# Moving the early weight splits and the first batch's routing to other slots of an attention pipeline, and dividing the weight conversions of the first experts differently

## The chip, the cores and the metric

The kernel runs on one core of a Trainium2 chip. TensorE (PE; its weight loads are PEld) multiplies matrices, VectorE (DVE), ScalarE (ACT) and GpSimd (POOL) do elementwise work, and SyncE (SP) starts most of the DMA transfers. The metric is the device time of one execution in microseconds (us).

## The reference

Three stages follow each other, all in float32:

```python
q_assign = argmax(normalised q @ normalised centroids)      # 16 clusters a head; k_assign alike
scores = where(q_assign == k_assign, q @ k.T / 8, -1e9)     # 2 batches x 8 heads, 768 x 768, D = 64
x = softmax(scores) @ v                                     # as 1536 tokens of 512
logits = normalised x @ normalised expert_emb.T / tau       # 8 experts
e = argmax(logits);  gate = softmax(logits)[e]
x = gate * (relu(x @ w1[e]) @ w2[e])                        # 512 -> 1024 -> 512, one expert a token
h = x @ w_in                                                # 512 -> 2048
out = (P(h) / (Q(h) + 1e-6)) @ w_out                        # P cubic, Q from |h| and h*h
```

## The kernel before, in words

The operands of most products are split into a high part in the type fp32r (hi) and a rest (lo = value - hi), and a product is made as hi x hi + lo x hi + hi x lo, or a part of that.

**Attention.** One unit is half of the queries (3 blocks of 128) of one head; there are 32 units. A unit has six key blocks kb, so the program runs through 192 slots t = 6 u + kb. Everything in a slot is written out by hand; `at(slot, function, ...)` puts other work into a slot. The order in a slot is: transposes of the probabilities into pt (L463), `word_high`, the exponential (L454), the parts phi and plo of the transposed block (L471 and L481 on ScalarE and VectorE; for kb = 0 GpSimd makes both, L72 and L479), the finishing of the unit before (px, L523), the other tasks, the products with v (L491, L492), and last one step of the running routing. The sums of a unit (ssum, L503) and the values' parts (vhl, L363) are GpSimd's too.

The transposes (pt), the scores (ps) and the output (po_acc) have PSUM banks of their own; one more bank, of the pool pM, is shared in turn by all that comes up rarely: the words (cm), the cluster logits (pl, L373 in the first two heads and L380 later) and the turned one-hots (po, L428), px, and the routing's products pr_ (L585) and ptab (L618). Who takes that bank has to wait until its user before has been read.

**Words.** The FFN's weights are prepared during the attention in 32 pieces ("words"): GpSimd makes the low half (L232, L234), ScalarE the high half into the bank cm (L239), VectorE joins the two into a buffer wz (L244), and a store writes it away. Two or three words fall to a period of 12 slots.

**Routing.** After the last head of a batch each half of the batch is routed to the experts: a chain of small VectorE operations (L563 to L580) makes a one-hot (rohb), TensorE counts the rank within the expert (pr_, L585), VectorE and GpSimd make J and at_row (L605 to L613), and TensorE turns them into the table of rows (ptab, L618). `advance_one` does the next step in chosen slots, steps that take the shared bank in slots of their own. The rows of x are stored to xd in DRAM as they are ready, and an indirect DMA on GpSimd (L658) gathers the rows of one expert by row_tok.

**Expert 0's first block.** The first 128 rows of expert 0 come from batch 0 alone, so they are worked on inside the end of the attention (names that begin with eb): `eb_gather`, `eb_ids`, `eb_x` (turned rows, ebx), `eb_in` (products with w1, L674, in the last eight slots and behind them), `eb_relu`, `eb_h`, `eb_low`, `eb_out` (products with w2, L689), `eb_end`. The weights come as four chunks of expert 0 (w1 in chunks 0 and 1, w2 in 2 and 3), each of 4 quarters of 128x512. `early_hi` makes a quarter's hi part, `early_lo` its lo part (L197), `early_split` both. `load_ahead(n)` starts the load of chunk n into one of three raw buffers (wraw, L129).

**The experts behind it.** `block_in`, `block_turn` (turned h; hhi L681, hlo L682) and `block_out` do expert 0's second 128 rows, `transpose_x(1)` turns expert 1's rows, and then a loop of steps (e = 1..7, p = 0..3) does the rest. `weights(k)` converts the next k quarters (ScalarE casts, L112, then VectorE subtracts, L117) into a ring of eight chunks. `row_gates` and `positions` are generators that the loop advances once a step; the second step of `positions` multiplies and copies the counts (pi, then pin, L1100). Afterwards comes the FFN, the second half of the run.

The lines that decide in which slots the routing of batch 0 advances, and where the early splits stand, are:

```python
            elif t % (2 * NB) in (1, 3, 7, 9):
                advance_one(t % (2 * NB) == 1)
            at((165, 170, 172, 177)[j], early_split, 0, j, pool, pool)
            at(186 + j, early_split, 1, j, act, pool)
            at(190 + j, early_hi, 2, j, act)
```

Of the kernel before, what the change touches and what calls it, by code (L numbers as in the profile page):

```python
# [10 lines left out]
F32 = mybir.dt.float32  # L11
# [10 lines left out]
P = 128  # L22
# [6 lines left out]
def attention_moe_kernel(ctx: ExitStack, tc: tile.TileContext, kqT, vp, centroids,  # L29
# [313 lines left out]
    def prep_split_first(i, qk):  # L343
# [11 lines left out]
        dve.tensor_copy(KB[D:P], qk[D:P])  # L355
# [77 lines left out]
    units = [(i, g) for i in range(NH) for g in range(2)]  # L433

# [81 lines left out]
    def finish(u):  # L516
        i, g = units[u]
        b, h = heads[i]
        px = (pS.tile([P, 3, D + E], F32, name="px", tag="ps") if u == n - 1 else
              pM.tile([P, 3, D + E], F32, name="px", tag="pm"))  # L520
        ob = st["ob", u]
        for j in range(3):
            pe.matmul(px[:, j, :], ob[:, j * P:(j + 1) * P], JE[:, h, :], start=True, stop=True)  # L523
        if h == 0 and g == 0:
# [12 lines left out]
        else:  # L537
            dve.tensor_tensor(x_sb[:, g * 3:g * 3 + 3, h * D:(h + 1) * D], px[:, :, 0:D],
                              r.to_broadcast([P, 3, D]), op=ALU.mult)
        if h == H - 2:  # L540
            dve.tensor_reduce(lg2[:, rows, :, 1], lg[:, rows], axis=AX.X, op=ALU.add)
            store_x(b, g, slice(0, h * D + D))
# [81 lines left out]
    def first_rows_1():  # L624
        tot = pM.tile([P, E], F32, name="ptot", tag="pm")
        pe.matmul(tot[:, 0:1], onesb, cum[:, 0:1], start=True, stop=True)
        dve.tensor_copy(e0[:, 0:1], tot[:, 0:1])
# [66 lines left out]
    def eb_gather():  # L694
        eb["x"] = hp.tile([P, S], F32, name="kq", bufs=4)[:, 0:W]
        gather_x(eb["x"], 0, NT // B + 1)

    def eb_ids():
        eb["y"] = hp.tile([P, S], F32, name="kq", bufs=4)[:, 0:W]
# [6 lines left out]
        eb["gates"] = gate(eb["gate"], eb["x"].unsqueeze(1), 1,  # L706
                           (ss, mx.unsqueeze(2), small[:, 128:128 + E].unsqueeze(1), sq))

    def eb_gate():
        next(eb["gates"], None)  # L710

    def eb_x():
# [4 lines left out]
        eb["ph"] = pS.tile([P, 2, 512], F32, name="ebh", tag="ps")  # L717

    def eb_in(j, first=0, upto=3 * KC):
        block_in(eb["ph"][:, j], eb["xT"], j, first, upto)  # L720

    def eb_relu(j):
        eb["hr", j] = hp.tile([P, 512], F32, name=f"wz{3 * j}", bufs=1)
        act.activation(eb["hr", j], eb["ph"][:, j], AF.Relu)
# [16 lines left out]
    def eb_end():  # L741
        act.activation(eb["y"][:, 0:DM], eb["o"], AF.Copy, scale=eb["gate"][:, 0:1])
# [39 lines left out]
    for j in range(15):  # L782
        for w0, w1_ in ((7, 11), (8, 17)) + (((9, 13),) if j in (9, 12) else ()):
# [32 lines left out]
    with tc.manual_schedule():  # L816
# [55 lines left out]
        cl_logits_first(1)  # L872
# [5 lines left out]
        cl_onehot(0)  # L878
        norm_1(embs, E, junk[:E, :], acc[:E, 2:3])
        cl_max(1)  # L880
        cl_transp_first(0)
# [70 lines left out]
        for j in range(4):  # L952
            at((165, 170, 172, 177)[j], early_split, 0, j, pool, pool)
# [640 lines left out]
```

## Time and profile before

| | |
|---|---|
| three runs | 770.41, 771.95, 773.9 us; median 771.95 |
| the profiled execution | 771.65 us, of which the span (first to last instruction) is 769.9 |
| attention | to about 305 us |
| experts | from there to about 500 us |
| FFN | to the end |

Busy time is the time in which an engine worked at an instruction. TensorE's matrix products are pipelined, so its instructions can overlap. A wait is idle time of an engine ahead of an instruction, with the instruction that ended it behind the arrow. The granted clock of a stretch is given as a share of full speed (1.00).

### The profile page before, as it was taken

Reading aid. Unit: us, or ns where it says so; the run is one execution under the profiler, and the core shown is the slowest. Engines: PE = TensorE matmul, PEld = TensorE weight load, DVE = VectorE, ACT = ScalarE, POOL = GpSimd, SP = SyncE. Lnnn points to the kernel's source line nnn. Section 1 sums busy time; section 2 is a strip of 40 time slices with the busy share of each in tenths; the row PEclk is TensorE's granted clock in tenths of the full one; section 3 lists DMA queues with packets and bytes.
Section 4 is the critical chain, followed back from the end, with each engine's and each line's share of the span. In section 5 each row is a group of like instructions: output and inputs, shape, how many; then the busy total and the mean of one; then the engine's idle time right before and its main releaser. Section 6 shows DMA issues by size and latency. Waiting matters only on the chain.

```text
span 769.9 us, 12566 instructions
## 1 busy us (share of the span) xinstructions
PE 734.6 (95%) x4261; PEld 636.2 (83%) x4261; DVE 591.5 (77%) x1125; ACT 567.1 (74%) x1131; POOL 368.0 (48%) x461
## 2 busy tenths in 40 slices
PE   6899999999999989989999999999999999999996
PEld 5789999998888877779889999878788888888885
DVE  6778888888898885578965655589987878788774
ACT  4778888888887893667875556588877677777774
POOL 7498888888777864102211012166544532242220
PEclk9999999999999999999999999999999999999999
DMA  5576776866777345479876656223000200010001
GB/s 146 158 205 176 197 218 195 241 183 211 237 251 242 101 161 169 149 277 321 264 265 199 213 184 202 82 77 103 14 1 14 69 16 13 0 56 1 0 1 58
DMA packets 48712, 109.20 MB, mean 142 GB/s; under 512 B 6937, under 2 KB 10777, under 8 KB 48642
## 3 DMA queue, kind: packets, MB, share of 16 engines
q1 hardware_dynamic: 45618, 98.65, 40.8%
q0 software_dynamic: 2880, 9.55, 4.2%
q8 instruction: 35, 0.57, 0.3%
q14 instruction: 35, 0.29, 0.1%
q10 hardware_dynamic: 144, 0.13, 0.1%
HBM read 76.06 MB, written 18.99 MB: 123 GB/s over the span
## 4 chain that ended last, share of the span: by engine, by line
PE 76%; DVE 8%; ACT 5%; issue 4%; DMA 3%; POOL 3%; SPq 0%; ACTq 0%; POOLq 0%; DVEq 0%
PE pg L1245 14%; PE ph L1174 9%; PE pt L463 6%; PE pr L1414 5%; PE pr L1412 5%; PE pr L1413 5%; PE po_acc L491 3%; PE ps L445 3%; PE ps L446 3%; PE po_acc L492 3%; PE py L1205 3%; PE py L1203 3%; PE py L1204 3%; PE px L523 3%; PE pl L380 2%
## 5 line engine op out<-in xcount | busy, mean ns | idle before, releaser
L1272 POOL TENSOR_TENSOR Bt<-Bt,A 128x512 f32<-128x512 f32 x46 | 59.7, 1298 | 147.2 <-ACT Bt L1270 147.2
L481 DVE TENSOR_TENSOR plo<-pt,phi 128x384 fp32r<-128x384 f32 x160 | 88.1, 551 | 24.2 <-ACT phi L471 21.8
L463 PE MATMUL pt<-ident,pr 128*128 128x128 f32 x576 | 96.2, 276 | 3.5 <-DVE plo L481 2.7
L471 ACT CAST phi<-pt 128x384 fp32r<-128x384 f32 x160 | 76.7, 482 | 30.9 <-PE pt L463 29.7
L448 DVE TENSOR_REDUCE nm<-ps 128x1 f32<-128x768 f32 x96 | 91.2, 950 | 5.4 <-PE ps L446 5.2
L1245 PE MATMUL pg<-x2hi,ck 128*128 128x512 f32 x368 | 92.7, 394 | 2.4 <-DVE Ct L1273 2.4
L454 ACT ACTIVATE pr<-ps,nm 128x768 f32<-128x768 f32 x96 | 87.3, 910 | 2.8 <-DVE nm L448 2.3
L1245 PEld LDWEIGHTS pg<-x2hi,ck 128*128 128x128 f32 x368 | 68.8, 188 | 19.1 <-DVE Ct L1273 3.7
L463 PEld LDWEIGHTS pt<-ident,pr 128*128 128x128 f32 x576 | 70.9, 140 | 16.4 <-DVE plo L481 7.1
L117 DVE TENSOR_TENSOR ck<-wraw,ck 128x512 fp32r<-128x512 f32 x112 | 70.8, 685 | 15.4 <-ACT ck L112 15.2
L1412 PE MATMUL pr<-ck,ghi 128*128 128x512 f32 x192 | 76.1, 396 | 0.0
L1414 PE MATMUL pr<-ck,glo 128*128 128x512 f32 x192 | 75.5, 393 | 0.0
L1413 PE MATMUL pr<-ck,ghi 128*128 128x512 f32 x192 | 75.3, 392 | 0.0
L491 PE MATMUL po_acc<-phi,vhl 128*128 128x384 f32 x192 | 73.4, 382 | 0.0
L640 POOL TENSOR_TENSOR gss<-gss,half 128x2 f32<-128x2 f32 (+1 forms) x8 | 6.2, 780 | 131.4 <-ACT px L639 114.9
L112 ACT CAST ck<-wraw 128x512 fp32r<-128x512 f32 x112 | 62.1, 624 | 9.4 <-DMA wraw<-in_w_dram 9.3
L492 PE MATMUL po_acc<-plo,vhl 128*128 128x384 f32 x192 | 65.0, 339 | 0.0
L1174 PE MATMUL ph<-xhi,ck 128*128 128x256 f32 x448 | 62.6, 282 | 0.0
L1389 DVE SCALAR_TENSOR_TENSOR Bt<-Bt,A 128x512 f32<-128x512 f32 (+1 forms) x48 | 32.7, 682 | 37.3 <-ACT A L1388 37.0
L1174 PEld LDWEIGHTS ph<-xhi,ck 128*128 128x128 f32 x448 | 59.0, 188 | 2.2
L1387 ACT ACTIVATE A<-Bt,qc 128x512 f32<-128x512 f32 (+1 forms) x48 | 34.3, 715 | 22.5 <-POOL Bt L1272 22.5
L1245 PE MATMUL pg<-x2lo,ck 128*128 128x512 f32 x184 | 49.9, 392 | 0.0
(328 smaller groups left out, 1941.1 us busy)
## 6 DMA issues: line engine op xcount, KB each, us to landing
wraw<-in_w_dram SPq DMA_DIRECT2D x32, 1024.0 KB, 5.8
words<-in_w_in_dram SPq DMA_DIRECT2D x16, 512.0 KB, 6.3
wf_d<-wz SPq DMA_DIRECT2D x32, 256.0 KB, 3.5
words<-in_w_out_dram SPq DMA_DIRECT2D x16, 512.0 KB, 5.2
yraw<-wf_d SPq DMA_DIRECT2D x16, 512.0 KB, 4.1
operands<-operands SPq DMA_DIRECT2D x40, 192.0 KB, 2.7
kq<-in_kqT_dram SPq DMA_DIRECT2D x16, 384.0 KB, 5.5
ys_d<-ysb SPq DMA_DIRECT2D x15, 260.0 KB, 3.8
```

Source lines behind the costliest of these rows:

```text
L448: dve.tensor_reduce(nm, ps[:, :, :HS], axis=AX.XY, op=ALU.max, negate=True)
L454: act.activation(pr.rearrange("p (a s) -> p a s", a=2), ps[:, :, :HS], AF.Exp, bias=nm[:, 0:1], accum_out=st["sum", u][:, qb:qb + 1])
L463: pe.transpose(t[:, j, :], st["P", u][j][:, kb * P:(kb + 1) * P], ident)
L471: act.copy(phi, tv)
L481: dve.tensor_tensor(plo, tv, phi.bitcast(F32), op=ALU.subtract)
L491: pe.matmul(o, w, phi, start=(kb == 1), stop=False)
L492: pe.matmul(o, w, plo, start=False, stop=(kb == 0))
L1174: pe.matmul(ph[:, f2, :], w[:, wx, k, c0:c0 + P], x[:, k, :], start=(i == 0), stop=(i == len(ops) - 1))
L1245: pe.matmul(ph, w[:, wx, k, c0:c0 + P], x[:, k, :], start=(i == 0), stop=(i == len(ops) - 1))
L1412: pe.matmul(o, ghi[:, s_], w[:, 0, k, :], start=(fb == 0), stop=False)
L1413: pe.matmul(o, ghi[:, s_], w[:, 1, k, :], start=False, stop=False)
L1414: pe.matmul(o, glo[:, s_], w[:, 0, k, :], start=False, stop=(fb == F2B - 1))
```

## The change

It moves work between slots and changes a few engines; nothing is computed differently.

1. At the start head 0's one-hot is turned (`cl_transp_first(0)`) ahead of head 1's cluster logits; the copy to KB goes from VectorE to ScalarE.
2. The two words of j = 14 (slots 168 to 187) are gone from there; two words more take third places in the periods j = 3 and 6, and join in slots 49 and 85, as others do at 121 and 157 already.
3. The routing of batch 0 advances in more slots: all odd ones but those of kb = 5, and t mod 12 = 4 and 10; steps that take the bank in t mod 6 = 1. By counting the steps, pr_ and ptab stand at slots 109 and 115 for the first half and 133 and 139 for the second (before: 121 and 133, 145 and 157). The count ptot is made in the bank of unit 22's px; the gather, ebx and the ids are 10, 11 earlier and 6 later (slots 147, 163, 165); the block's gate leaves the slots and goes behind the attention as `eb_gate_1` to `_3`.
4. Chunk 0 is split at slots 165, 167, 170, 173; chunk 1 wholly on GpSimd at 175 to 181 (before: ScalarE and GpSimd at 186 to 189); chunk 2's hi on ScalarE at 183 to 187, its lo on GpSimd at 184 and 186 and on VectorE at 187 and 188; chunk 3's lo on VectorE behind the gate. Load 3 is at slot 174, loads 4 and 5 at 187 and 191, load 6 ahead of `eb_out(0, 8)`.
5. The rows x and y of expert 0's block lie in a tile of their own (spare_x), the halves of its h in two PSUM tiles (ebh), and the final scale goes to VectorE.
6. Behind the attention 16 quarters are converted ahead of the loop of steps, before 8; the generator `positions` starts its second step at i = 5, before at i = 2.

```diff
-        dve.tensor_copy(KB[D:P], qk[D:P])
+        act.copy(KB[D:P], qk[D:P])
...
+        bank_ = (pS.tile([P, 512], F32, name="px", tag="ps") if u == n - 1 else
+                 pM.tile([P, 512], F32, name="px", tag="pm"))
+        px = bank_[:, 0:3 * (D + E)].rearrange("p (j d) -> p j d", d=D + E)
...
+        if u == UF:
+            tot = bank_[:, 500:501]
+            pe.matmul(tot, onesb, cum[:, 0:1], start=True, stop=True)
...
     def eb_gather():
-        eb["x"] = hp.tile([P, S], F32, name="kq", bufs=4)[:, 0:W]
+        spare = xpool.tile([P, NB, W], F32, name="spare_x", tag="x_sb")
+        eb["x"], eb["y"] = spare[:, 0], spare[:, 1]
...
+    def eb_gate_1():
+        ss, mx, v, sq = eb["gates"]
+        act.activation(sq, eb["x"][:, 0:DM], AF.Square, accum_out=ss)
+        pool.tensor_tensor(ss, ss, half, op=ALU.pow)
+
+    def eb_gate_2():
+        ss, mx, v, sq = eb["gates"]
+        dve.tensor_reduce(mx, eb["x"][:, DM:W], axis=AX.X, op=ALU.max)
+        dve.tensor_tensor(v, eb["x"][:, DM:W], mx.to_broadcast([P, E]), op=ALU.subtract)
+        dve.tensor_scalar(ss, ss, 1e-6, None, op0=ALU.add)
+        dve.reciprocal(ss, ss)
...
     def eb_in(j, first=0, upto=3 * KC):
-        block_in(eb["ph"][:, j], eb["xT"], j, first, upto)
+        if first == 0:
+            eb["ph", j] = (pT if j else pS).tile([P, 512], F32, name="ebh", tag="pt" if j else "ps")
+        block_in(eb["ph", j], eb["xT"], j, first, upto)
...
-        act.activation(eb["y"][:, 0:DM], eb["o"], AF.Copy, scale=eb["gate"][:, 0:1])
+        dve.tensor_scalar(eb["y"][:, 0:DM], eb["o"], eb["gate"][:, 0:1], None, op0=ALU.mult)
...
-    for j in range(15):
-        for w0, w1_ in ((7, 11), (8, 17)) + (((9, 13),) if j in (9, 12) else ()):
+    for j in range(14):
+        for w0, w1_ in ((7, 11), (8, 17)) + (((9, 13),) if j in (3, 6, 9, 12) else ()):
...
-            at((165, 170, 172, 177)[j], early_split, 0, j, pool, pool)
-            at(186 + j, early_split, 1, j, act, pool)
-            at(190 + j, early_hi, 2, j, act)
-        for j in range(2):
-            at(192 + j, early_lo, 2, j, pool)
-            at(T + j, early_hi, 3, j, act)
-        at(178, load_ahead, 3)
-        at(134, first_rows_1)
-        at(136, first_rows_2)
-        at(157, eb_gather)
-        at(159, eb_ids)
...
+            at((165, 167, 170, 173)[j], early_split, 0, j, pool, pool)
+            at((175, 177, 179, 181)[j], early_split, 1, j, pool, pool)
+            at((183, 185, 186, 187)[j], early_hi, 2, j, act)
+            at((184, 186, 187, 188)[j], early_lo, 2, j, dve if j > 1 else pool)
+        at(174, load_ahead, 3)
+        at(187, load_ahead, 4)
+        at(191, load_ahead, 5)
...
+            elif t % 2 and t % NB != 5 or t % (2 * NB) in (4, 10):
+                advance_one(t % NB == 1)
...
+        weights(4)
         block_in(ph[0], x1, 0)
         act.activation(hr[0], ph[0], AF.Relu)
-        weights(2)
+        weights(1)
         block_in(ph[1], x1, 1, 0, 6)
         block_turn(0)
+        weights(2)
         block_in(ph[1], x1, 1, 6)
...
-            if i == 1:
+            if i == 4:
                 later.append(place_rows)
```

GpSimd, the last slots of the attention before: the five subtractions in a row (ck with its number is one chunk; 4461 is chunk 1, 4533 chunk 2), then the routing's J.

```order
L503 TENSOR_SCALAR ssum<-ssum 128x3
L72 TENSOR_SCALAR phi<-ptc 128x384
L479 TENSOR_TENSOR plo<-ptc,phi 128x384
L197 TENSOR_TENSOR ck_4461<-wraw,ck_4461 128x512 x4
L197 TENSOR_TENSOR ck_4533<-wraw,ck_4533 128x512
L612 TENSOR_TENSOR rJ<-rot,rsec 128x24
L613 TENSOR_TENSOR rJ<-rot,rJ 128x24
```

The same place of the changed kernel (4267 is chunk 1, 4412 chunk 2; its lines are numbered a few higher):

```order
L72 TENSOR_SCALAR ck_4267<-wraw 128x512
L197 TENSOR_TENSOR ck_4267<-wraw,ck_4267 128x512
L504 TENSOR_SCALAR ssum<-ssum 128x3
L197 TENSOR_TENSOR ck_4412<-wraw,ck_4412 128x512
L72 TENSOR_SCALAR phi<-ptc 128x384
L480 TENSOR_TENSOR plo<-ptc,phi 128x384
L197 TENSOR_TENSOR ck_4412<-wraw,ck_4412 128x512
L619 TENSOR_TENSOR rJ<-rot,rsec 128x24
```

Chunk 1 has moved ahead, hi parts and all, and one subtraction of chunk 2 stands between the last phi/plo pair and J.

VectorE, from the last unit but one's finishing to the one-hot of the last but one routing, before:

```order
L481 TENSOR_TENSOR plo<-pt,phi 128x384 x2
L531 TENSOR_TENSOR lg_2678<-px,rr 128x24
L538 TENSOR_TENSOR x_sb<-px,rr 128x3x64
L563 TENSOR_TENSOR x_sb<-lg_2678 128x3x8
L567 TENSOR_REDUCE rmx<-x_sb 128x3
L569 TENSOR_TENSOR rv<-x_sb,rmx 128x24
```

And after:

```order
L197 TENSOR_TENSOR ck_4412<-wraw,ck_4412 128x512
L501 TENSOR_SCALAR ssum<-ssum 128x3
L509 RECIPROCAL rr<-ssum 128x3
L482 TENSOR_TENSOR plo<-pt,phi 128x384
L197 TENSOR_TENSOR ck_4412<-wraw,ck_4412 128x512
L482 TENSOR_TENSOR plo<-pt,phi 128x384
L536 TENSOR_TENSOR lg_2697<-px,rr 128x24
```

Two subtractions of chunk 2 have come in between the plo operations, ahead of the routing; before they stood behind row_tok.

VectorE in the loop of steps around the copy to pin, before:

```order
L117 TENSOR_TENSOR ck_5087<-wraw,ck_5087 128x512 x2
L650 TENSOR_SCALAR gate<-gmx_4900 128x2
L651 RECIPROCAL gate<-gate 128x2
L1100 COPY pin<-px_5094 128x8
L666 TENSOR_TENSOR xlo<-px_5132,xhi 128x4x128
```

And after:

```order
L117 TENSOR_TENSOR ck_5266<-wraw,ck_5266 128x512 x2
L117 TENSOR_TENSOR ck_5304<-wraw,ck_5304 128x512
L1204 SCALAR_TENSOR_TENSOR hlo<-ph,hhi 128x512
L117 TENSOR_TENSOR ck_5304<-wraw,ck_5304 128x512 x3
L1121 COPY pin<-px_5335 128x8
```

The copy still stands behind weight subtractions, but of a later chunk, three steps later in the loop.

## Rows read from the trace of the kernel before

**Rows 1.** The page, TensorE: busy time, share of the span, instructions.

```profile
PE 734.6 (95%) x4261; PEld 636.2 (83%) x4261; DVE 591.5 (77%) x1125; ACT 567.1 (74%) x1131; POOL 368.0 (48%) x461
```

**Rows 2.** Windows of units: length; busy us and instructions of each engine; clock; DMA.

```profile
91.00:97.90 6.90, 6.90 (x49) 6.58 (x48) 6.18 (x14) 6.81 (x17) 5.58 (x13) 1.00 0.75 220
...
97.90:107.01 9.11, 9.10 (x67) 8.32 (x66) 7.17 (x14) 7.21 (x17) 8.45 (x12) 1.00 0.58 168
...
272.71:279.70 6.99, 6.89 (x47) 6.18 (x46) 6.42 (x15) 6.65 (x17) 2.44 (x4) 1.00 0.87 284
```

**Rows 3.** TensorE's waits: total us, times, longest.

```profile
PE px L664 <- DVE pin L1100: 2.9, 1, 2.9
...
PE pr__4558 L585 <- DVE rohb L577: 2.8, 1, 2.8
...
PE pr__3024 L585 <- DVE wz L244: 1.4, 1, 1.4
...
PE ptab L618 <- DVE wz L244: 1.4, 1, 1.4
...
PE py L689 <- ACT hhi L681: 1.1, 1, 1.1
...
PE ebh L674 <- ACT wz L724: 0.7, 1, 0.7
...
PE px L523 <- DVE e L627: 0.6, 1, 0.6
...
PE ebx L664 <- PE ps L446: 0.6, 1, 0.6
```

**Rows 4.** Timelines of the start: start, length, engine, line, operands, [idle before].

```profile
10.46 2.77 PE L373 MATMUL pl<-CB,kq 128*128 128x32 f32 x12 [1.37 <-POOL kq L324]
...
11.73 0.28 ACT L411 ACTIVATE oh<-oh 128x96 bf16<-128x96 bf16 x1
...
13.16 1.45 PE L428 MATMUL po<-identb,oh 128*16 128x128 bf16 x12
...
33.22 0.83 POOL L324 TENSOR_SCALAR kq<-kq 64x768 f32<-64x768 f32 x1 [5.62 <-DMA kq<-in_kqT_dram]
```

**Rows 5.** Groups by line: busy us, mean ns of one, idle before.

```profile
L197 POOL TENSOR_TENSOR ck<-wraw,ck 128x512 fp32r<-128x512 f32 x12 | 15.1, 1279 | 0.3
...
L197 DVE TENSOR_TENSOR ck<-wraw,ck 128x512 fp32r<-128x512 f32 x4 | 2.6, 687 | 0.0
...
L72 POOL TENSOR_SCALAR ck<-wraw 128x512 fp32r<-128x512 f32 x4 | 2.5, 620 | 0.2
...
L232 POOL TENSOR_SCALAR wz<-words 128x512 f32<-128x512 f32 x32 | 21.0, 656 | 1.3
...
L234 POOL TENSOR_SCALAR wz<-words 128x512 uint16<-128x512 uint16 x32 | 25.0, 780 | 2.6
...
L239 ACT ACTIVATE cm<-words 128x512 f32<-128x512 f32 x32 | 20.6, 645 | 2.5 <-DVE x_sb L538 2.5
```

**Rows 6.** Timelines of VectorE and GpSimd at 282 to 296 us.

```profile
285.28 0.99 DVE L569 TENSOR_TENSOR rv<-x_sb,rmx 128x24 f32<-128x24 f32 x1
...
295.82 0.18 DVE L569 TENSOR_TENSOR rv<-x_sb,rmx 128x24 f32<-128x24 f32 x1
...
282.46 6.22 POOL L197 TENSOR_TENSOR ck<-wraw,ck 128x512 fp32r<-128x512 f32 x5
```

**Rows 7.** Windows of 5 us at the end of the attention and behind it.

```profile
290.00:295.00 5.00, 4.31 (x19) 3.21 (x17) 1.44 (x8) 1.08 (x2) 4.43 (x5) 0.70 0.01 2
...
315.00:320.00 5.00, 5.00 (x27) 4.12 (x27) 2.88 (x5) 3.28 (x7) 0.00 (x0) 1.00 0.02 3
```

**Rows 8.** ScalarE's timeline behind the attention.

```profile
312.83 0.59 ACT L681 CAST hhi<-px 128x512 fp32r<-128x512 f32 x1 [2.02 <-DMA ys_d<-kq]
...
336.53 1.66 ACT L112 CAST ck<-wraw 128x512 fp32r<-128x512 f32 x3 [4.08 <-DMA wraw<-in_w_dram]
```

More of the change, by code (lines that the diff above doesn't have):

```diff
@@ L433, in attention_moe_kernel @@
     units = [(i, g) for i in range(NH) for g in range(2)]
+    UF = 22
     def scores(u, qb):
@@ L622, in route, with first_rows_1 @@
             dve.tensor_tensor(table, table, pt_, op=ALU.add)
[L624 to L627, printed above, removed]
+    def first_rows_1(tot):
+        dve.tensor_copy(e0[:, 0:1], tot)
         dve.tensor_scalar(e0[:, 1:2], e0[:, 0:1], -1.0, float(P), op0=ALU.mult, op1=ALU.add)
@@ L705, in eb_ids, with eb_gate_3 @@
         sq = hp.tile([P, S], F32R, name="ot", bufs=1)[:, 0:DM].bitcast(F32)
[L706 to L710, printed above, removed]
+        eb["gates"] = (ss, mx, small[:, 128:128 + E], sq)
+    def eb_gate_1():
[8 more added lines that the diff above has]
+        dve.reciprocal(ss, ss)
+    def eb_gate_3():
+        ss, mx, v, sq = eb["gates"]
+        act.activation(v, v, AF.Exp, scale=ss[:, 0:1], accum_out=mx)
+        dve.tensor_scalar(eb["gate"], mx, 1e-9, None, op0=ALU.add)
+        dve.reciprocal(eb["gate"], eb["gate"])
     def eb_x():
@@ L972, in attention_moe_kernel @@
                 transp(u, kb)
+            if t == 141:
+                assert not running
             for fn, args in todo:
@@ L1001, in attention_moe_kernel @@
             if T - NB <= t <= T:
-                advance(2)
-                advance(2)
-            elif t % (2 * NB) in (1, 3, 7, 9):
-                advance_one(t % (2 * NB) == 1)
+                for _ in range(2 if t < T - 1 else 1):
+                    advance(2)
+            elif t % 2 and t % NB != 5 or t % (2 * NB) in (4, 10):
+                advance_one(t % NB == 1)
         eb_in(0, 10)
         eb_relu(0)
+        advance()
         eb_in(1, 0, 2)
@@ L1010, in attention_moe_kernel @@
         eb_in(1, 2, 4)
-        advance()
-        assert not running
         r = route(B - 1, 1)
@@ L1015, in attention_moe_kernel @@
         eb_h(0)
-        eb_in(1, 4, 8)
-        load_ahead(4)
-        early_lo(3, 0, pool)
-        early_lo(3, 1, pool)
-        for _ in range(5):
-            next(r)
-        eb_in(1, 8)
+        eb_in(1, 4, 7)
+        for _ in range(4):
+            next(r)
+        while running:
+            advance()
+        eb_gate_1()
+        next(r)
+        eb_in(1, 7)
         eb_relu(1)
+        early_hi(3, 3, act)
         eb_out(0, 0, 4)
         next(r)
-        early_hi(3, 2, act)
         eb_low(0)
+        eb_gate_2()
         next(r)
         next(r, None)
-        early_hi(3, 3, act)
         eb_h(1)
         eb_out(0, 4, 8)
-        early_lo(2, 2, dve)
-        early_lo(2, 3, dve)
         eb_low(1)
+        eb_gate_3()
+        for j in range(4):
+            early_lo(3, j, dve)
+        load_ahead(6)
         eb_out(0, 8)
-        for j in range(2, 4):
-            early_lo(3, j, dve)
         eb_out(1)
@@ L1319, in attention_moe_kernel @@
         place_rows = positions()
-        next(later[0])
         next(place_rows)
@@ L1330, in attention_moe_kernel @@
             passed.add(("in", e, p))
+            if i == 0:
+                expert_relu(e, p)
             weights(3)
@@ L1336, in attention_moe_kernel @@
                         transpose_y(0, 2 * (p - 2) + tb, x2b)
-            if e < E - 1:
+            if 0 < i and e < E - 1:
                 expert_relu(e, p)
```

26 lines of the change are left out of this document (15 added, 11 removed).

## The prediction

> **What bounds the kernel now.** I read the page first, then the list of TensorE's waits, then windows cut at the attention units, and the timelines where a wait was long. TensorE works 734.6 us of a span of 769.9 [rows 1], so all its pauses together are 35.3 us, and a change that adds no arithmetic to TensorE can only remove pauses, add some, or move the clock. The windows of ten us show TensorE pausing before 350 us, and behind that only in two places of the FFN which the edit does not come near; so what is won early should be kept. In the attention an even unit takes 6.90 us and an odd one 9.11 with TensorE never idle; the even unit is also nearly full on ScalarE, 6.81 of 6.90 [rows 2]. The list of waits [rows 3] says where units that take longer lose their time, and its lines are the stock that this change can draw on.
>
> **How the time is counted.** The profiled execution took 771.65 us, 1.75 of it outside the span; the median of the three runs is 771.95, 0.3 more. I sum against 771.65 and compare with the median. Half a per cent of it is 3.9 us, about what a measurement of this kernel can tell from no change.
>
> **The start.** Head 1's cluster logits (L373), 2.77 us on a TensorE not yet at speed, ran from 10.46 us, and head 0's one-hot turn (L428) behind them until 14.61 [rows 4]. Now the turn comes first. Its one-hot is ready at 12.01, so it ends at 13.46, the logits at 16.23, and head 0's first scores, which need the turn alone but stand behind both, come 1.6 us later. What covers this: GpSimd stood 5.62 us, until 33.22, for a key load that the new order does not delay, and TensorE's next units were waiting for it [rows 4]. The KB copy costs ScalarE what it frees on VectorE. I take 0; bounds -0.3 (the cover is whole and head 1 starts sooner) and +1.6 (no cover).
>
> **Two more third words, at slots 49 and 85.** One costs GpSimd 0.66 + 0.78, and ScalarE 0.65 [rows 5]. ScalarE has 0.1 to spare in an even unit [rows 2], but the odd unit behind it has 1.9, so most of 2 x 0.65 is made up: +0.3, bounds 0 and +1.3. In return two words are gone from slots 168 to 187, 2 x 1.44 of GpSimd's time among them, where it is wanted.
>
> **The routing of batch 0.** Before, a routing step took the shared PSUM bank in slots 121 and 157, and in exactly these slots the third word used it first: TensorE stood 1.4 us behind the word's join (wz) each time. The first transposes of expert 0's block (ebx) and the product for px cost 0.6 each [rows 3]. Afterwards the bank is taken in slots 109, 115, 133 and 139, where no word uses it, the count rides in the bank of px, and ebx stands at slot 163. Four waits go, 4.0 us. Against that, the steps' small VectorE operations delay some plo in their new units, and ScalarE there has 0.1 us to spare [rows 2]; for that I give back one wait as long as ebx's and a little, 0.8. Net -3.2; bounds -1.4 (one of the two long waits and more is replaced by new ones) and -4.0.
>
> **The end of the attention, 285 to 305 us.** TensorE waits 2.8 us for rohb [rows 3]. The wait is made on VectorE: a routing operation on 128x24 takes 0.99 us at 285.28 while GpSimd is inside five splits of 1.28 each, and the same line takes 0.18 at 295.82 when it is idle [rows 6]. Three such operations stand in the chain, 0.8 lost in each, 2.4. After the pause the granted clock is 0.70 from 290 to 295 us, a mixture of the two levels, 2.4 and 1.2 GHz, with 4.31 us of work [rows 7]: that costs 0.30 x 4.31 = 1.3. Afterwards chunk 1 is done on GpSimd in slots 175 to 181 and only two subtractions of chunk 2 are left for it at 184 and 186, so it should be through before the routing step at about slot 190. Two more products stand ahead of the waiting one as well. The wait for wz on the shared ebh tile, 0.7, ends because the halves have tiles of their own. That is 2.8 + 1.3 + 0.7 = 4.8 to win. Is there room on GpSimd? Eight whole splits at 0.62 + 1.28 and two subtractions are 17.8 us in slots 165 to 187, where four splits and two words were 7.6 + 2.9 before: 7.3 more. The unit at 272.71 used 2.44 of 6.99 [rows 2], which gives 4.5, and the five splits that ran at 282.46 [rows 6] leave the place after it. It fits with about 1 us left. Costs that come back: the last pr_ now stands right behind ptab in the same bank, with VectorE's table addition between them (0.2 plus two hand-overs, 0.4), and the four gate operations and the gate's second half come ahead of row_tok and the last chunk's subtractions (four of 0.69 on VectorE), which their consumer eby reaches about when they end. Together +0.8. Net -4.0; bounds -1.0 (only the 0.7 and a little go) and -4.8.
>
> Two subtractions of chunk 2 are VectorE's own, beside GpSimd's. The Trainium skill (SBUF — State Buffer, "Who interferes with whom") says that a VectorE instruction with two SBUF inputs and a GpSimd instruction that reads SBUF shut each other out, whichever comes second waiting for all of the first. The trace agrees as far as it goes: 0.99 against 0.18 [rows 6]. By that rule each of the two could stand behind a GpSimd split.
>
> **Behind the attention, 305 to 345 us.** Two waits stand out there: 1.1 for hhi and 2.9 for pin [rows 3]. The first came from a tile that the store of expert 0's rows was still reading: ScalarE waited 2.02 on that DMA [rows 8]. The rows now lie in the tile spare_x, so hhi needs no store. The 2.9 came because VectorE's copy of pin was queued behind weight subtractions, these behind ScalarE's casts, and those 4.08 us behind a weight load [rows 8]. Meanwhile the DMA engines were busy 0.02 of the time at 315 to 320 [rows 7]: the loads had been held back for conversions that hold the raw buffers. Now loads 4 and 5 go out at slots 187 and 191, load 6 before the block's last products, and 16 quarters are converted ahead of the loop instead of 8, eight casts and eight subtractions more of at most 0.69 us each [rows 5], in a stretch where ScalarE works 3.28 and VectorE 2.88 of 5 us [rows 7]. The product of pi and its copy move from the loop's step 2 to step 5. Both go: -4.0; bounds -2.5 (pin's wait comes back at step 5 at half its size) and -4.6 (a few waits of 0.3 or so, not listed, go as well).
>
> **Sum.** 0 + 0.3 - 3.2 - 4.0 - 4.0 = -10.9; 771.65 - 10.9 = 760.75, or 11.2 below the median. All good bounds together are -0.3 + 0 - 4.0 - 4.8 - 4.6 = -13.7 (758.0), all bad ones 1.6 + 1.3 - 1.4 - 1.0 - 2.5 = -2.0 (769.7).
>
> **The rivals.**
> - GpSimd is not through in time: pr_ waits about as long as before, and the clock falls. For it: 1 us of room is little, and GpSimd's subtraction at slot 186 queues behind a phi/plo pair. Against it: two words are gone from there. The end gives 0.5 instead of 4.0: 764.3.
> - VectorE's two subtractions of chunk 2, at slots 187 and 188, queue behind GpSimd's, as its routing operation at 285.28 seems to have done [rows 6]: 1.28 each, 2.6 of the end's 4.0, 763.4. It takes a GpSimd subtraction under way when each starts, and plo standing behind them.
> - The routing lands in slots as full as the old ones: ScalarE's 6.81 of 6.90 speaks for it; that the two 1.4 us waits had a cause which is gone speaks against it. Then -3.2 becomes 0: 764.0.
> - The weight loads still rule after the attention, and the pin copy meets the same queue at step 5: for it speaks that the 4.08 us wait was for a load's data, against it that the DMA engines had stood idle shortly before. Then -4.0 becomes -1.1: 763.7.
> - Slower: GpSimd's splits hold up phi, plo and the sums of each unit from slot 165 on. A phi/plo pair behind one whole split is 1.9 us late, a sum behind a subtraction 1.28, 3.2 per unit; over four and a half units that is 14, and with the rest of the gain 771.65 + 14 - 6.9 = 778.8 (the rest of the gain is 0.3 - 3.2 - 4.0). It decides from the point at which GpSimd's queue is longer than its unit; my count leaves it 1 us short of that, and a backlog in one unit alone only costs 3.2.
>
> **How the numbers follow.** The forecast has 0.48. The first rival 0.10, the second 0.07, the third 0.10, the fourth 0.09: all these are faster by more than 0.5%, 0.84 together. Two of them at once leave 4.2 to 5.4 of the gain, at the edge; with the start's 1.6 on top, or three at once, less than 3.9: 0.11, the same. The slower one has 0.05. For 8 in 10 the range goes from 756.5 (pauses that I left out of the sum give more) to 768: the last 0.16 lie mostly above.
>
> **What would show it.** In the trace after: no wait for wz before pr_ or ptab, each 1.4; the routing operations at about 285 us near 0.2 us and pr_'s wait below 0.5; a granted clock of 0.95 or more from 285 to 295; hhi not behind a DMA; pin without a wait; the DMA engines busy at 310 to 320; TensorE's idle time down from 35.3 to about 26 (the 1.3 of the clock isn't idle time). I am wrong if GpSimd's subtractions of chunk 2 still run when the routing starts, if plo waits grow in slots 165 to 187, or if the gather of the first rows is late, since it hangs on row_tok, whose chain has four more VectorE operations ahead of it.

## The result, and the profile after

The changed kernel takes 763.46 us (median of 11 executions, 762.09 to 770.3), the kernel before 771.95 (11 executions, 769.0 to 775.05). The ratio over all executions is 0.9906, 95% interval 0.9878 to 0.9934; by the medians alone it is 0.9890. The forecast was 760.75, and the range 756.5 to 768 holds the median. The profiled execution took 764.09 us with a span of 762.4, 7.5 less than the span of before.

The page's line on the engines, beside [rows 1]: TensorE's work is the same within 0.7 us, so its pauses went from 35.3 to 28.5 us.

```profile
PE 733.9 (96%) x4261; PEld 636.5 (83%) x4261; DVE 594.5 (78%) x1127; ACT 565.0 (74%) x1127; POOL 368.0 (48%) x463
```

TensorE's waits after, beside [rows 3] (total us, times, longest):

```profile
PE pt L464 <- DVE plo L482: 4.9, 9, 1.0
PE po L428 <- ACT oh L410: 2.5, 1, 2.5
PE po_acc L493 <- DVE plo L482: 1.0, 1, 1.0
PE px L669 <- DMA xr<-xd,row_tok: 0.9, 1, 0.9
PE pl L380 <- DVE table L629: 0.7, 2, 0.4
PE pe L933 <- DVE early L928: 0.6, 1, 0.6
PE pr__4643 L592 <- DVE table L629: 0.3, 1, 0.3
```

All eight lines of [rows 3] are gone. The waits for plo went from seven, 2.7 us together, to ten, 5.9; a gather costs 0.9, and a one-hot at the start 2.5 (no wait in the profile before; 1.35 in one other profile with the old start). Two waits for the table's addition (L629) are new; they stand ahead of cluster logits, which need the same bank.

Windows after: three attention units, as in [rows 2], the last five slots of the attention, and stretches of 5 us as in [rows 7]:

```profile
89.25:96.62 7.37, 7.06 (x49) 6.57 (x48) 6.89 (x15) 7.30 (x18) 6.71 (x14) 1.00 0.75 173
162.13:172.45 10.32, 9.30 (x67) 8.30 (x66) 9.35 (x19) 7.30 (x17) 8.93 (x13) 1.00 0.73 204
272.24:280.09 7.85, 6.99 (x46) 6.23 (x46) 5.84 (x14) 6.73 (x16) 7.37 (x9) 1.00 0.40 150
280.09:286.40 6.31, 5.70 (x36) 4.81 (x37) 5.12 (x13) 3.76 (x8) 3.87 (x4) 1.00 0.80 265
...
290.00:295.00 5.00, 4.74 (x32) 4.03 (x30) 3.45 (x18) 2.98 (x8) 1.62 (x5) 1.00 0.73 229
...
315.00:320.00 5.00, 5.00 (x41) 4.87 (x40) 4.52 (x16) 3.52 (x10) 0.90 (x2) 1.00 0.69 239
```

From 290 to 295 us the granted clock is 1.00 where it was 0.70, and from 315 to 320 the DMA engines are busy 0.69 of the time where it was 0.02 [rows 7]. But units take longer than 6.90 and 9.11 us [rows 2]: the one at 89.25 has a third word, the one at 162.13 a routing step, the last two have the splits.

Where the 7.5 us came from, place by place. The program is followed by its marks: the first transposes of each unit, the last product of expert 0's block, the first step of the expert loop. Each row gives the time of the stretch before and after, and the difference:

```
stretch                                       before   after    diff.
to unit 8 (start, units 0 to 7)                91.00   89.25    -1.75
units 8 to 15 (the new third words)            64.09   65.99    +1.90
units 16 to 26 (routing of batch 0)            94.36   94.50    +0.14
unit 27 to slot 191 (early splits)             35.45   36.66    +1.21
slot 191 to the end of expert 0's block        19.58   15.10    -4.48
from there to the loop's first step            16.00   14.13    -1.87
from there to the end of the span             449.42  446.77    -2.65
```

### The profile page after: what moved, and what is told of

Its sections match the earlier page's. It is cut to its first block, busy times and chain, and to the rows that moved or that the text cites. A ratio compares the mean times of both kernels' runs of the same rounds, so it can differ in the third digit from the quotient of the medians.

```text
span 762.4 us, 12565 instructions
## 1 busy us (share of the span) xinstructions
PE 733.9 (96%) x4261; PEld 636.5 (83%) x4261; DVE 594.5 (78%) x1127; ACT 565.0 (74%) x1127; POOL 368.0 (48%) x463
## 4 chain that ended last, share of the span: by engine, by line
PE 75%; DVE 12%; ACT 5%; issue 4%; POOL 2%; DMA 1%; POOLq 0%; ACTq 0%; DVEq 0%; SPq 0%
PE pg L1266 14%; PE ph L1195 9%; PE pt L464 5%; PE pr L1441 5%; PE pr L1439 5%; PE pr L1440 5%; PE ps L446 3%; PE po_acc L492 3%; PE py L1226 3%; PE py L1225 3%; PE py L1224 3%; PE ps L447 3%; PE po_acc L493 3%; PE pl L380 2%; PE px L525 2%
```

## The experiments

Each run is compared with executions of the kernel before on the same chip. The slots and names are those of the sections above.

**What the new start does.** The kernel before with the start's order and KB's copy alone changed:

```diff
-        dve.tensor_copy(KB[D:P], qk[D:P])
+        act.copy(KB[D:P], qk[D:P])
...
-        cl_logits_first(1)
...
-        norm_1(embs, E, junk[:E, :], acc[:E, 2:3])
-        cl_max(1)
         cl_transp_first(0)
+        cl_logits_first(1)
+        cl_max(1)
+        norm_1(embs, E, junk[:E, :], acc[:E, 2:3])
```

> The kernel before with the start alone changed (head 0's one-hot turn ahead of head 1's logits, the KB copy on ScalarE). Theory: the changed order itself brings the start forward, through an earlier chain to the fourth key load; then unit 4 starts some 1.7 us earlier than before (58.98), at about 57.2, and the time falls by 1.7 to about 770.2. Rival: the first key transfer merely landed earlier by chance in the profile after; then GpSimd's first norm starts at about 9.5 again, unit 4 within 0.5 us of 59, and the time stays at 772 or is up to 1.6 worse.

Measured: 773.31 against 771.65, 1.0023 (0.9995 to 1.0051). Nothing is won, though unit 4 began 2.3 us earlier in its profile. The same lines put back in the changed kernel:

> The changed kernel with the old order at the start. The runs of the kernels with the new order fall into two groups some 5 us apart (761.5 to 763.2 and 766.8 to 769.8 in the run with the old routing slots), and in a profile of the later group unit 0 takes 10.93 instead of 7.64 us. Theory: the new order makes the start a matter of chance; with the old one unit 4 starts at about 59.0 as before, the times lie within 3 us of each other, about 765, and the group at 767 and above is gone. Rival: the two groups come from behind the start (clock, transfers); then the times still fall into two groups and the median is 1.7 us above the changed kernel's.

Measured: 764.06 (762.12 to 765.27, 6 executions), 0.9918 (0.9899 to 0.9936). Unit 4 starts at 56.76, earlier than in the changed kernel (57.24) and than before (58.98), with the order of before. So the 1.75 us at the top of the list need not be the new order's. They are not shown to be chance either: in the other six profiles with the old order unit 4 starts at 57.7 to 59.0, with the new order at 56.6 to 57.2 in three profiles and at 59.5 to 64.1 in four, which the last run below explains in part.

**Where the routing stands.** The changed kernel with the routing, the gather, the count and ebx in their slots of before:

```diff
-            elif t % 2 and t % NB != 5 or t % (2 * NB) in (4, 10):
-                advance_one(t % NB == 1)
+            elif t % (2 * NB) in (1, 3, 7, 9):
+                advance_one(t % (2 * NB) == 1)
...
-        at(144, first_rows_2)
-        at(147, eb_gather)
-        at(163, eb_x)
-        at(165, eb_ids)
+        at(134, first_rows_0)
+        at(136, first_rows_2)
+        at(157, eb_gather)
+        at(159, eb_ids)
+        at(174, eb_x)
```

> The changed kernel with the routing of batch 0 and the block's gather, ids and turn back in their old slots. Theory: the new slots won nothing, since the two waits of 1.4 us that went were replaced by waits for plo behind the routing's VectorE operations; slot 191 then stands within 1 us of the changed kernel's 286.4, the time within 1 us of 763.5, and the list of waits has wz before pr_ and ptab again, 1.4 each. Rival: the new slots do win the 3.2 us of the prediction, and something else in the attention loses them; slot 191 comes at about 289.5 and the time is about 766.7.

Measured: 764.99 (761.46 to 769.82), 0.9915 (0.9884 to 0.9945): as good as the changed kernel. Its waits show the old ones back:

```profile
PE pr__3038 L592 <- DVE wz L244: 1.4, 1, 1.4
PE ptab L625 <- DVE wz L244: 1.4, 1, 1.4
PE ebx L669 <- PE ps L447: 0.8, 1, 0.8
...
PE px L525 <- DVE e L632: 0.6, 1, 0.6
```

and units 16 to 26 take 94.69 us with three of these waits, 3.4 us (the one before ebx stands in unit 29), 94.50 without them. The new slots take back what they save.

**The early splits.** The changed kernel with the splits and loads 3 to 6 where they were (other lines of the block's end move with them):

```diff
-            at((165, 167, 170, 173)[j], early_split, 0, j, pool, pool)
-            at((175, 177, 179, 181)[j], early_split, 1, j, pool, pool)
-            at((183, 185, 186, 187)[j], early_hi, 2, j, act)
-            at((184, 186, 187, 188)[j], early_lo, 2, j, dve if j > 1 else pool)
-        at(174, load_ahead, 3)
-        at(187, load_ahead, 4)
-        at(191, load_ahead, 5)
+            at((165, 170, 172, 177)[j], early_split, 0, j, pool, pool)
+            at(186 + j, early_split, 1, j, act, pool)
+            at(190 + j, early_hi, 2, j, act)
+        at(178, load_ahead, 3)
```

> The changed kernel with the early splits of chunks 1 to 3 and the loads 3 to 6 back in their old places. Theory: the moved splits cost about 1.2 us up to slot 191 and win some 4.5 behind it; here slot 191 comes at about 285.2, the routing operation after the last but one unit takes about 0.9 us again, pr_ waits over 2 us, the granted clock falls behind it, and the time is 3 to 4 us longer, about 767. Rival: the separate ebh tiles and the new order behind the attention did it; then pr_ waits below 0.5 and the time stays near 763.5.

Measured: 769.01 (765.82 to 774.48), 0.9968 (0.994 to 0.9995), 5.5 us above the changed kernel by medians, 4.8 by the ratios. Its profile has the price and the return apart. Windows of its units 29 and 30 and of the five slots behind them, in which TensorE is never idle:

```profile
263.85:270.81 6.96, 6.96 (x49) 6.51 (x48) 6.28 (x14) 6.14 (x15) 4.32 (x6) 1.00 0.11 40
270.81:277.50 6.69, 6.69 (x48) 6.27 (x47) 5.49 (x12) 6.03 (x14) 1.72 (x3) 1.00 0.80 260
277.50:282.69 5.19, 5.19 (x37) 4.89 (x36) 3.10 (x9) 4.61 (x12) 3.97 (x5) 1.00 0.35 133
```

18.84 us, where the changed kernel needs 21.38 from 265.02 to 286.40: the splits in their new slots cost 2.5 there. From slot 191 to the end of expert 0's block this run needs 19.1 us, the changed kernel 15.1. Behind slot 191 its waits are, beside 1.5 us for plo:

```profile
PE px L669 <- DMA xr<-xd,row_tok: 1.9, 2, 1.2
PE pr__4554 L592 <- DVE rohb L584: 1.6, 1, 1.6
PE pr__4640 L592 <- DVE table L629: 1.3, 1, 1.3
```

The other way round, the kernel before with the new word places, the splits of chunks 0 to 2 and load 3 alone:

> The kernel before with the new word places and the new slots of the early splits of chunks 0 to 2 and of load 3, all else old. Theory: the splits lose some 2.5 us up to slot 191 and end the wait for rohb, 2.8, and the fall of the clock behind it, 1.3 or more; the pause at pin stays. Time 1 to 2 us below before, about 770. Rival: the gain behind slot 191 needs the separate ebh tiles and the early loads, and the chunk's late parts hold up eby or the gather instead; the time is that of before or above.

Measured: 770.37, 0.9991 (0.9972 to 1.001). Alone they bring nothing. Units 8 to 15 and unit 27 to slot 191 took 66.4 and 37.0 us, 2.3 and 1.5 more than before; pr_'s wait fell from 2.8 to 0.7 and pin's from 2.9 to 1.6, 3.4 together. From the end of the block to the loop's first step the profile took 14.3 us for 16.0 before. But the granted clock still fell:

```profile
290.00:295.00 5.00, 3.74 (x20) 2.71 (x18) 2.44 (x12) 1.15 (x3) 3.19 (x4) 0.92 0.02 3
295.00:300.00 5.00, 5.00 (x26) 4.16 (x25) 2.47 (x14) 1.31 (x4) 0.23 (x1) 0.74 0.29 41
```

The last two columns show no load going out in 290 to 295, where the changed kernel has a share of 0.73.

Two kernels vary the engines of the new splits. Chunk 1's hi parts on ScalarE, in the same slots of the changed kernel:

```diff
-            at((175, 177, 179, 181)[j], early_split, 1, j, pool, pool)
+            at((175, 177, 179, 181)[j], early_split, 1, j, act, pool)
```

> The changed kernel with chunk 1's hi parts made on ScalarE, in the same slots 175 to 181: 4 x 0.62 us less for GpSimd. Theory: the 2.5 us that units 29 to 31 lose against the run with the old splits come from GpSimd's backlog (VectorE waits 1.65 for a sum, and its next operation on sums takes 1.24); then slot 191 comes 1 to 2 us earlier and the time is about 762. Rival: ScalarE is as full there, phi comes later, and nothing is won: slot 191 within 0.5 us of 286.4 or later.

Measured: 764.8 (761.92 to 772.14), 0.9927 (0.9904 to 0.9951). Unit 30 takes 7.03 us instead of 7.86, but the median is no better. VectorE's two subtractions of chunk 2 behind the attention:

```diff
-            at((184, 186, 187, 188)[j], early_lo, 2, j, dve if j > 1 else pool)
+            if j < 2:
+                at((184, 186)[j], early_lo, 2, j, pool)
...
+        early_lo(2, 2, dve)
+        early_lo(2, 3, dve)
         eb_low(1)
```

> The changed kernel with VectorE's two subtractions of chunk 2 back behind the attention. Theory: of the loss of units 29 to 31 they are the smaller part; slot 191 comes some 0.7 to 1.4 us earlier, and eby's products then wait about as long for them, so the time is within 1 us of 763.5. Rival: they hold up plo and the routing behind them by more than their length; the time is 2 us less.

Measured: 774.98 (771.96 to 782.63), 1.0054 (1.0023 to 1.0085): slower than the kernel before. What it saves in the last five slots is 0.9 us (5.38 for 6.31). What it costs stands in its waits, in SyncE's timeline and in the windows:

```profile
PE px L669 <- DMA xr<-xd,row_tok: 7.3, 1, 7.3
```

```profile
300.89 0.38 SPq L129 DMA_DIRECT2D wraw<-in_w_dram  x1
301.37 0.45 SPq L514 DMA_DIRECT2D xd<-x_sb  x1
```

```profile
305.00:310.00 5.00, 0.00 (x0) 0.00 (x0) 0.36 (x1) 0.00 (x0) 2.12 (x2) 0.71 1.03 338
310.00:315.00 5.00, 2.47 (x7) 1.88 (x8) 1.37 (x3) 1.99 (x4) 1.00 (x1) 0.50 0.45 144
```

Load 5 needs chunk 2's raw buffer, which the two late subtractions still read. It stood at the head of SyncE's queue until 300.89, and the store of the last rows of x behind it went out 0.5 later; in the changed kernel both left by 292.51. The gather of expert 1's rows waits for that store, TensorE for the gather, and behind the pause the clock stood at 0.50. Neither theory had this.

**Behind the attention.** The kernel before with the new conversions behind the attention (weights in the block's products, pin at step 5), without the early loads of the slots:

```diff
+        weights(4)
...
-        next(later[0])
...
-            if i == 1:
+            if i == 4:
                 later.append(place_rows)
```

> The kernel before with only the part behind the attention changed (16 quarters converted ahead of the loop, the count of rows in step 5, the order in step 0). Theory: this alone ends the wait for pin, 2.9 us, while the 1.1 us wait for hhi behind the store stays; the time is about 768.8. Rival: without the loads 4 and 5 issued in the attention the weight transfers still rule, and the waits come back at casts and hhi; then the time is within 1 us of 772.

Measured: 768.06 (767.08 to 771.44), 0.9956 (0.9936 to 0.9975), by the ratio 3.4 us won. And the last of these lines alone:

> The kernel before, only with the count of rows moved from step 2 to step 5 of the loop. Theory of the prediction: the pause at pin came because the weights were late, so moving the count alone leaves TensorE waiting at another place of the same stretch (a weight or hhi) or moves the pause to step 5; the gain is below 1.5 us, time 770.5 or more. Rival: the pause belongs to the copy's place in VectorE's queue alone; then it goes, 2.9 us and the clock falls behind it with it, and the time is 768.1 as in the run with all of the part behind the attention.

Measured: 769.16 (766.59 to 771.82), 0.9974 (0.9958 to 0.9989). Pin's wait of 2.9 is gone and no other stands in its place: the copy waited for its place in VectorE's queue, and three steps later in the loop nothing waits for it. By the ratio that is 2.0 of the 3.4 us. That the other 1.4 are the conversions' is not shown, and the profiles speak against it: from the end of expert 0's block to the end of the span the kernel before takes 465.4 us, this run 462.7 and the run with the conversions 462.9. The two runs differ ahead of that stretch, where the clock in this one stood at 0.51 and 0.50 from 290 to 300, in the other at 0.74 and 1.00.

**Two tries at a better kernel.** The old start and chunk 1's hi on ScalarE together, and the same with the routing's steps in other slots:

> The changed kernel with the old order at the start and chunk 1's hi parts on ScalarE, the two edits that removed something alone. Theory: the group of slow starts goes, and units 29 to 31 lose 0.8 us less than in the changed kernel; the times lie close together with a median of about 763, within 1 us of the changed kernel's best group. Rival: the gain of 0.8 is given back behind slot 191; median 764.

Measured: 764.04 (762.99 to 765.85, 6 executions), 0.991 (0.9883 to 0.9936): the changed kernel's time with less spread.

```diff
-            elif t % 2 and t % NB != 5 or t % (2 * NB) in (4, 10):
+            elif t % (2 * NB) in (1, 3, 4, 5, 7, 9):
```

> As the run with the old start and ScalarE's hi parts, with the routing of batch 0 advanced in slots 1, 3, 4, 5, 7 and 9 of 12 instead of 1, 3, 4, 7, 9 and 10: one step in the even unit, where GpSimd works less, in place of one in the odd unit. Theory: the 1.0 us pauses of the odd units 17 and 21 come from routing operations that stand behind GpSimd's; they shrink, and unit 27 starts 1 to 2 us earlier. Rival: the pauses come from VectorE's load as such; they move to the even units and unit 27 starts within 0.5 us of the other run.

Measured: 768.88 (767.37 to 771.75), 0.9966 (0.9946 to 0.9987), 4.8 worse. A rank count (pr_) now takes the shared bank just ahead of a head's cluster logits (L380), which need the same bank. TensorE's timeline in unit 19:

```profile
184.46 0.17 PE L597 MATMUL pr__2899<-cum,onesb 128*128 128x24 bf16 x1
184.48 0.53 PE L464 MATMUL pt<-ident,pr 128*128 128x128 f32 x3
186.35 2.57 PE L380 MATMUL pl<-CB,kq 128*128 128x32 f32 x12 [1.35 <-DVE rrk L599]
```

It stood 1.35 us for VectorE's reading of the bank, and then the same twelve products that took 1.42 in the kernel before took 2.57, at a lower granted clock (0.65 here, 0.66 up to 195):

```profile
185.00:190.00 5.00, 3.65 (x17) 3.68 (x17) 2.46 (x8) 1.83 (x5) 3.54 (x7) 0.65 0.97 245
```

That unit took 14.25 us, the next but one 13.43, where the kernel of the run above needed 10.15 and 10.33.

**The same kernel again.** The changed kernel had given two groups of times, so it was run once more unchanged:

> The changed kernel once more, beside the others on one chip. Theory: two groups of times again, about 763 and 767 to 770, and a median between 763 and 766; units 17, 19, 21 and 23 take 10.1 to 10.4 us as in its first profile. Rival: the first profile's long units were chance; then they differ by more than 0.5 us.

Measured: 766.8 (762.62 to 771.29, 6 executions). Of the 17 executions now there, nine took 762.1 to 764.1 us and eight 766.7 to 771.3. This profile took 771.29. Its units 17, 19, 21 and 23 took 10.32, 10.16, 10.37 and 10.24 us, as in the first profile; what is different is the start. VectorE's timeline, and GpSimd's:

```profile
31.66 3.00 DVE L928 TENSOR_SCALAR early<-early,acc,itau 8x512 f32<-8x512 f32 x2
```

```profile
30.69 0.83 POOL L324 TENSOR_SCALAR kq<-kq 64x768 f32<-64x768 f32 x1 [0.78 <-DMA kq<-in_kqT_dram]
31.61 0.83 POOL L72 TENSOR_SCALAR operands<-kq 128x768 fp32r<-128x768 f32 x1
32.53 1.85 POOL L330 TENSOR_TENSOR operands<-kq,operands 128x768 fp32r<-128x768 f32 x1
```

TensorE's waits and its windows in the same execution:

```profile
PE pe L933 <- DVE early L928: 2.7, 1, 2.7
```

```profile
30.00:35.00 5.00, 2.28 (x16) 1.74 (x15) 5.00 (x7) 2.57 (x7) 3.52 (x3) 0.97 0.51 171
35.00:40.00 5.00, 5.00 (x23) 4.78 (x23) 2.41 (x4) 1.68 (x5) 1.95 (x3) 0.50 0.36 79
```

L928, two small operations, takes 3.00 us when GpSimd's key operations are under way, and ends 0.28 behind the last of them. In the profile of the changed kernel shown first it was through 0.07 us before they began:

```profile
29.88 0.98 DVE L928 TENSOR_SCALAR early<-early,acc,itau 8x512 f32<-8x512 f32 x2
```

```profile
30.93 0.83 POOL L324 TENSOR_SCALAR kq<-kq 64x768 f32<-64x768 f32 x1 [1.85 <-DVE early L928]
```

It started 1.05 us ahead of them there and 0.97 behind them here.

What makes L928 late stands ahead of it in TensorE. The cluster logits of one head and VectorE's first operation on them, in the execution of 771.29:

```profile
22.73 2.60 PE L380 MATMUL pl<-CB,kq 128*128 128x32 f32 x12
```

```profile
25.72 0.35 DVE L387 TENSOR_REDUCE mx<-logits 128x12 f32<-128x192 f32 x1 [1.79 <-ACT logits L383]
```

The same products in the profile of 764.09:

```profile
22.69 1.79 PE L380 MATMUL pl<-CB,kq 128*128 128x32 f32 x12
```

They take 1.42 us in all seven profiles with the old start. With the new one they take 1.42, 1.76 and 1.79 in the three profiles in which L928 takes 0.98, and 2.60 in the four others, about what they took at the granted clock of 0.65 above (2.57). In these four TensorE kept that pace up to 26 to 30 us, although the column of the clock has 1.00 from 20 to 30, and VectorE's queue, with L928 in it, was late. With the new start TensorE stands 2.47 us for the one-hot ahead of all this in every profile, with the old one 1.35 in one profile and not at all in six. What decides when the pace rises stays open, and no run moved L928 alone.

With the start of before, L928 starts at 27.35 to 28.39 us and the key operations at 31.03 to 33.22, in all seven profiles that have it: 2.8 us apart or more. With the new start it takes 3.00 in three of seven profiles (the runs with the routing's old slots, with the subtractions behind the attention, and this one), and 1.50 in a fourth (the one with chunk 1's hi parts on ScalarE). Here unit 4 starts at 64.10, 6.9 later than in the profile of 764.09, and the execution ends 7.2 later. In the run with the routing's old slots it took 3.00 as well, but the clock stayed at 1.00; unit 4 came 3.9 later, and the execution took 767.78. The slower group has these two steps, six executions from 766.7 to 767.5 and two at 770.3 and 771.3; only one execution of it has a profile, so for the first step the cause goes by the other kernel. Twelve executions with the old start (the runs of 764.06 and 764.04) are all between 762.1 and 765.9.

## Why the prediction was right, and where not

The direction, the range and three of the mechanisms were right. The sum was 3.3 us too good against its own profiled time (764.09 for 760.75), and this is how it falls on the terms:

- **The start: 0 forecast, within a profile -1.75 to +5.1.** As a median the term is near 0: the start alone gave 1.0023, and undoing it 0.9918 for 0.9906. But the argument, GpSimd's wait for the key load as cover, missed what moves with the order: TensorE stands 2.47 us for the one-hot and in four of seven profiles works at the slow pace for longer, and L928 comes into GpSimd's key operations. What the new order brings is a chance of 4 or 7 us; the -1.75 of this profile is luck as far as the forecast goes. For the chance speak the profiles, and that the slower group is absent in 12 executions without the new order.
- **Two more third words: +0.3 forecast, +1.9 in this profile.** The unit at slot 49 took 0.47 longer, as the range had it; the units around slot 85 took 7.71 and 9.76 instead of 6.97 and 9.08. The odd unit was to make the time up and had 1.9 us of ScalarE's time to do so; it lost 0.7 instead. In other profiles of the same slots these two units lose 0.4 to 3.1. Of the ten profiles with these slots, units 8 to 15 lose 0.8 to 0.9 in four, within the bound of 1.3, and 1.5 to 3.6 in six, this one among them. The size was wrong, the bound held in four of ten; what makes the difference stays open.
- **The routing of batch 0: -3.2 forecast, +0.14 measured. This is the step that failed,** and the third rival (that the steps land in slots as full, 764.0) came true, though by VectorE's queue and not by the full ScalarE that it named; that the time fits its 764.0 is chance, since words, splits, start and end cancel. The four waits did go, three of them, 3.4 us, in these units; the fourth, ebx's 0.6, stood in unit 29, and with it the term is -0.4. The step said: "the steps' small VectorE operations delay some plo in their new units", and gave 0.8 for it. Four odd units (17, 19, 21 and 23) took 10.32, 10.14, 10.34 and 10.21 instead of 9.12, 9.21, 9.20 and 9.09, 4.4 together. In 17 and 21 TensorE waits 1.0 for plo; into 19 and 23 have come ptab's own product, 0.4, and 0.35 for the table's addition. Over units 16 to 26 the waits for plo grew from 1.5 to 3.9 us and those for the table from nothing to 0.7, so TensorE's idle time only went from 4.9 to 4.6. VectorE's timeline in the unit at 197.83, GpSimd's, and TensorE's:

```profile
198.61 1.04 DVE L584 TENSOR_TENSOR rohb<-rv,rm 128x24 bf16<-128x24 f32 x1
199.68 0.44 DVE L585 CAST oh_all<-rohb 128x24 f32<-128x24 bf16 x1
200.15 0.18 DVE L587 TENSOR_TENSOR rot<-oh_all,tok 128x24 f32<-128x24 f32 x1
200.25 0.55 DVE L482 TENSOR_TENSOR plo<-pt,phi 128x384 fp32r<-128x384 f32 x1
```

```profile
197.77 1.83 POOL L330 TENSOR_TENSOR KA<-kq,operands 128x768 fp32r<-128x768 f32 x1
```

```profile
200.86 0.44 PE L493 MATMUL po_acc<-plo,vhl 128*128 128x384 f32 x1 [0.97 <-DVE plo L482]
```

L584 works on 24 numbers a partition and takes 1.04 us until GpSimd's operation is through, 0.18 at 288.02 where GpSimd stands still. The plo behind it in the queue is late, and TensorE waits 0.97. I had this row in hand, [rows 6], and used it for the end of the attention only; the odd units are GpSimd's fullest, 8.45 of 9.11 [rows 2]. The Trainium skill (SBUF — State Buffer, "Who interferes with whom") has the one that comes second wait for all of the first. The trace agrees: 1.04 ends at 199.65, and GpSimd's at 199.60.
- **The splits before slot 191: not in the sum, +1.2 against before, +2.5 against the old splits.** (The run with the old splits is itself 1.3 quicker there than the kernel before: two words and ebx's wait have left this stretch.) The check that GpSimd's work fits had GpSimd's time alone. It fitted: its last subtraction of the attention ended at 284.60, before the routing's first operation at 286.61. But phi, plo and the sums stood behind the splits, the mechanism of the slower rival at a small part of its 14 us. VectorE's timeline and GpSimd's at its last split:

```profile
283.38 1.24 DVE L501 TENSOR_SCALAR ssum<-ssum 128x3 f32<-128x3 f32 x1
```

```profile
282.87 1.73 POOL L197 TENSOR_TENSOR ck<-wraw,ck 128x512 fp32r<-128x512 f32 x1
```

Three numbers a partition take 1.24 us, and GpSimd's subtraction 1.73 instead of 1.28, beside VectorE's own of chunk 2: the second rival's collision happened, in the sums and not in chunk 2, for about 1 us.
- **The end of the attention: -4.0 forecast, -4.48 measured.** Right in each step: the routing's operations took 0.18 us again at 287 us (0.99 in [rows 6]), pr_ behind ptab waited 0.26, the forecast's 0.4, the clock stayed at 1.00, and wz's wait is gone. With the old splits and loads the two pr_ wait 1.6 and 1.3 again, and with the new splits alone the wait for rohb falls from 2.8 to 0.7: that the splits' new places end most of it is shown. The clock needs more than them: with the splits alone it was 0.92 and 0.74.
- **Behind the attention: -4.0 forecast, -4.5 measured to the end of the span.** Hhi no longer waits for a DMA, pin not at all. That the pin copy's place in the loop ended its wait is shown (2.0 us alone by the ratio). From the end of the block to the end of the span the changed kernel takes 460.9 us, 1.8 less than with the pin copy alone (462.7). The conversions without the early loads bring none of this (462.9); with the old splits and loads, all else as in the changed kernel, 1.5 of it is lost (462.4), 1.2 as a wait for a gather. What the early loads give alone was not run.

So, by stretches, the miss of 3.3 is the routing's 3.3, the words' 1.6 and the splits' 1.2, less the start's 1.75 and the 1.0 that the two stretches behind slot 191 gave over the forecast. A version that is clearly better than the changed kernel was not found; with the old start it is as quick, and takes 762 to 766 us instead of 762 to 771.

## What to carry to other kernels

A wait that goes from the list is worth only what its new place leaves: price the moved work where it arrives, and above all who stands behind it in the same engine's queue there. A small VectorE operation is not small while GpSimd is in a long one, so put such chains where GpSimd is idle, as at the end of the attention here, not where TensorE has a hole. And two groups of times for one kernel are a finding: profile one execution of each, and look for two operations that come within a microsecond of each other.

## What was not expected of the hardware

- **A pause is not always followed by a lower clock.** Behind the same wait of 2.8 us before pr_ the granted clock from 290 to 295 was 0.70 before, 0.51 with pin moved, 0.50 with the new start alone, 0.74 with the new conversions; behind pauses of 1.6 and 1.3 with the old splits it was 1.00. Behind pin's wait, 2.9 before and 3.1 with the new start alone, it was 1.00 before from 340 to 350, and 0.57 with the new start from 345 to 350. And a pause of 1.35 us, in the run of 768.88, was followed by 0.65. So a pause has no one price: with the same wait of 2.8 the stretch from slot 191 to the end of expert 0's block took 19.6 us before, 22.7 with pin moved, 22.5 with the new start alone and 19.6 with the new conversions.
- **The column of the clock does not show all of it.** The twelve products L380 of one head took 1.42 us at 21.40 with the old start, and 1.79 at 22.69 and 2.60 at 22.73 in two executions with the new, all in windows at 1.00. What made them slower there stays open.
- **Operations with one input in SBUF are held up beside GpSimd too:** L928 3.00 for 0.98, L585 0.44 for 0.18, and L501 1.24 for 0.16 with three numbers a partition. I had counted only those with two.
- **The key load of the start** let GpSimd begin at 30.69 to 31.09 us in six profiles, and at 31.28 to 33.22 in the other eight. Five of the six have the new start, and six of the eight the old one, so the order seems to play a part; how is open, and with it the 1.75 us at the top of the list.
